# Whole-token stacks of queries and keys, a value product in one part, and a new spread of w_in's splitting steps

## The chip, the core and the metric

The kernel runs on one core of one Trainium2 chip, with its five engines: PE (matrix products, with PEld for the loading of weights), DVE (vector), ACT (scalar functions), POOL (a second, slower vector engine) and SP, which here only issues transfers. The metric is the device time of one launch in microseconds (us). Three runs of the kernel before took 1129.81, 1126.02 and 1126.63 us, median 1126.63. Trace times below count from the start of the profiled span.

## The reference

One block of a network on x of 2048 tokens by 640 features: attention with a sliding window of 256 tokens and 32 heads of 20 features, and then a gated mixer.

```python
def _A_ref(x, wqkv, wo):
    H = 32; Dh = D // H; W = 256
    qkv = (x @ wqkv) as [3, B, H, S, Dh]
    scores = einsum("bhqd,bhkd->bhqk", q, k) * Dh ** -0.5
    mask = (idx[:, None] - idx[None, :] >= 0) & (idx[:, None] - idx[None, :] < W)
    p = softmax(where(mask, scores, -1e9))
    return einsum("bhqk,bhkd->bhqd", p, v) as [B, S, D] @ wo

def _B_ref(x, w_in, w_sp, b_sp, w_out):
    z = gelu(x @ w_in); z1 = z[..., :864]; z2 = layernorm(z[..., 864:])
    g = w_sp @ z2 + b_sp[:, None]
    return (z1 * g) @ w_out

h = x + _A_ref(layernorm(x), wqkv, wo)
h2 = h + _B_ref(layernorm(h), w_in, w_sp, b_sp, w_out)
```

## The kernel before, in words

**Stages.** The first 60 us hold the layer norm and v. From there to about 237 us come the dense products for queries and keys (`qk_item`, products on L568 to L570): each 128 x 512 result is split into three bf16 parts (L584 to L592, the splits of which DVE, ACT and POOL make one each) and stored to DRAM as `qk_d` (L595). From 238 to about 470 us runs the attention loop, from 466 to 558 us the 16 iterations of the product with wo, and then the mixer's products, up to the end.

**Stacks.** The heads stand in 8 groups of 4. For a group `load_stack` (L298) makes a *stack*: 120 partitions with six copies of bf16 parts of 20 features, so that one bf16 product over 120 rows gives a score that is nearly f32, and three further rows (120 to 122) that carry the negative row maxima on the side of the queries and ones on the side of the keys. A stack is two tiles, one for each half of the tokens (`b`). Each holds queries (`a` = 0) and keys (`a` = 1) of the four heads. There are three slots for stacks, `slot_0` (first slot), `slot_1` (second) and `xb`; in names of the order below the pairs of tiles are `slot_0_99`, `slot_1_100`; `slot_0_1950`, `slot_1_1951`; `xb_94`, `xb_95`, the half b = 0 first. 24 loads (L311: half b, part j, side a, in this nesting) fill a stack. The ones are set by POOL (L304), for the first three groups only.

**The attention loop** has steps s = 0 to 129, 16 for each group. For each of the four heads of a step s, in this order: `max_item(s + 16)` makes the product of 128 queries with their window of keys in four strips (L341) for the row maxima, which DVE takes (L351); `score_item(s)` makes 128 keys by 384 queries (L394), here with the maxima's rows in the product, and ACT takes the exponential (L397), POOL masks it (L401, L404); and `pv_item(s - 2)` makes the product with v and the row sum (L422) in two parts, the first after head 1, the second after head 3. Every second step its result is evicted (L438 on ACT, L440 on DVE) and stored to `o_d` (L441). So group g's maxima are made in the 16 steps before its scores; for group 0 in the dense stage, there as a single product of 128 queries (L345).

**The maxima's way.** After 8 query blocks `max_rows` transposes 32 columns of maxima on PE (L357), which DVE and POOL split in three bf16 rows; SP stores them to `m_d` (L366) and loads them into rows 120 to 122 of the stack (L368). For the second token half of group g that begins in step 16g, after head 1.

**What sets the order.** PE, DVE, ACT and SP take their instructions in the written order of the program; a tile framework adds the waits, from which tile an instruction reads or writes and where. SP issues nearly all transfers, each in its turn. In the wo loop (L1300 on) a generator `w1` makes one splitting step of w_in for each `next`, one an iteration and a second one where a list of iterations says so.

Of the kernel before, what the change touches and what calls it, by code (L numbers as in the profile page):

```python
# [7 lines left out]
F32 = mybir.dt.float32  # L8
F32R = mybir.dt.float32r
BF16 = mybir.dt.bfloat16  # L10
# [5 lines left out]
P = 128  # L16
S = 2048
D = 640
H = 32
DH = 20  # L20
# [8 lines left out]
ONES = 1.0019378662109375  # L29
# [5 lines left out]
def block_kernel(ctx, tc, x, xt, wqk, wv, wo, w_in, wsp, bsp, w_out, out):  # L35
    nc = tc.nc
# [201 lines left out]
    with ExitStack() as ab:  # L238
# [14 lines left out]
        slot_w, slot_ap = {}, {}  # L253

        def add_slot(i, halves):

            slot_ap[i] = [h.bitcast(BF16).rearrange("p (a h t) -> p a h t", a=2, h=4) for h in halves]
# [40 lines left out]
        def load_stack(g):  # L298


            st = slot_w[g % 3]
            if g < 3:
                for h in st:
                    nc.gpsimd.memset(h[96:P, 1], ONES)  # L304
                    if g == 2:
                        yield
            for b in range(2):
                for j, parts in enumerate(((0, 0), (0, 1), (0, 2), (1, 0), (1, 1), (2, 0))):
                    for a in range(2):
                        src = qk_d[g // 4, parts[a], b, a * DH:(a + 1) * DH, g % 4 * 4:g % 4 * 4 + 4]  # L310
                        nc.sync.dma_start(st[b][j:6 * DH:6, a], src)  # L311
# [11 lines left out]
        def one(st, rows, a, hh, t0, n):  # L323
            (_, _, x), = tokens(st, rows, a, hh, t0, n)
            return x

        def max_item(g, qb, hh, strips=True):

            st = slot_ap[g % 3]
            ps = s1_tile()  # L330
            lo = max(0, qb - 2) * P
            n = (qb + 1) * P - lo
            keep = mask[:, 384 - n:]
            if strips:
                skip = 32 if qb > 1 else 0
                if skip:
                    n, keep = 288, strip
                for j in range(4):
                    q0 = qb * P + 32 * j
                    for o, w, k in tokens(st, 120, 1, hh, lo + skip * j, n):  # L340
                        nc.tensor.matmul(ps[32 * j:32 * j + 32, o:o + w], one(st, 120, 0, hh, q0, 32), k,  # L341
                                         start=True, stop=True, tile_position=(0, 32 * j))
            else:
                for o, w, k in tokens(st, 120, 1, hh, lo, n):
                    nc.tensor.matmul(ps[:, o:o + w], one(st, 120, 0, hh, qb * P, P), k, start=True, stop=True)  # L345
            b, c = divmod(qb, 8)
            if c == 0 and hh == 0:
                m_cols[g, b] = tmp2.tile([P, 32], F32, tag="mcol", bufs=2, name=f"mcol{g}_{b}")
            junk = tmp2.tile([P, 384], BF16, tag="junk", bufs=2, name=f"junk{g}_{qb}_{hh}")
            c += hh * 8  # L350
            nc.vector.tensor_tensor_reduce(out=junk[:, :n], in0=ps[:, :n], in1=keep, scale=1.0,  # L351
                                           scalar=NEG, op0=OP.add, op1=OP.max, accum_out=m_cols[g, b][:, c:c + 1])

        def max_rows(g, b):

            ps = s1_tile()[:32, :P]
            nc.tensor.transpose(ps, m_cols.pop((g, b)), ident)  # L357
# [8 lines left out]
            nc.sync.dma_start(rows.rearrange("a r c -> r a c"), m3.bitcast(F32))  # L366
            yield
            nc.sync.dma_start(slot_w[g % 3][b][120:123, 0], rows.rearrange("a (h r) c -> a h (r c)", h=4))  # L368
            yield

        p_tiles, pv_tiles = {}, {}
# [1 line left out]
        def score_item(u, hh):  # L373


            g, kb = divmod(u, NT)
            st = slot_ap[g % 3]
            n = min(384, S - kb * P)
            if hh == 0:
                p_tiles[u] = tmp3.tile([P, 4, 384], F32, tag="pt", bufs=4, name=f"pt{u}")  # L380
            pt = p_tiles[u]
            if u > NU - LEAD:
                if hh % 2 == 0:
                    bank2.append(bank2.pop(0))
                ps = bank2[-1][:, hh % 2]
            else:
                ps = s2_tile()
            for i in range(4):
                k0 = kb * P + 32 * i
                b, e = 32 * i, min(n, 32 * i + 288)  # L390
                if NU - LEAD < u and 4 * (u - NU + LEAD - 1) + hh < 6:
                    b, e = 0, n
                for o, w, q in tokens(st, 123, 0, hh, kb * P + b, e - b):
                    nc.tensor.matmul(ps[32 * i:32 * i + 32, b + o:b + o + w], one(st, 123, 1, hh, k0, 32), q,  # L394
                                     start=True, stop=True, tile_position=(0, 32 * i))
            if u <= NU - LEAD:
                nc.scalar.activation(pt[:, hh, :n], ps[:, :n], AF.Exp, scale=SCALE)  # L397
# [46 lines left out]
        if True:  # L444
# [134 lines left out]
            def split_qk(m, c, ps):  # L579
                sg = tmp.tile([P, 3, 512], BF16, tag="ta", bufs=3, name=f"sg{m}_{c}")  # L580
                rest = tmp.tile([P, 512], F32, tag="tb", bufs=2, name=f"rest{m}_{c}")
                nc.vector.tensor_tensor(out=rest, in0=ps, in1=stds[c], op=OP.mult)
                yield
                nc.scalar.activation(sg[:, 0, :], rest, AF.Copy)  # L584
                yield
                (nc.gpsimd if m > 5 else nc.vector).tensor_tensor(out=rest, in0=rest, in1=sg[:, 0, :],
                                                                  op=OP.subtract)
                if (m, c) == (9, 3):
                    nc.gpsimd.tensor_copy(out=sg[:, 1, :], in_=rest)
                else:  # L590
                    nc.scalar.activation(sg[:, 1, :], rest, AF.Copy)
                nc.gpsimd.tensor_tensor(out=sg[:, 2, :], in0=rest, in1=sg[:, 1, :], op=OP.subtract)  # L592
                T = S // 4
                base = qk_d[m // 5, 0, c // 2, m % 5 * 8, 0, c % 2 * 256:c % 2 * 256 + 256]
                nc.sync.dma_start(bass.AP(tensor=base.tensor, offset=base.offset,  # L595
                                          ap=[[T, P], [2 * 2 * DH * H // 2 * T, 3], [1, 256]]), sg.bitcast(F32))

            halves = [slice(0, HD), slice(HD, D)]
            load_x(0)
# [711 lines left out]
    for i in range(1, NT + 1):  # L1311
# [95 lines left out]
```

## Time and profile before

| what | value |
|---|---|
| median of 3 runs | 1126.63 us |
| profiled execution | 1125.76 us |
| its span | 1124.0 us |
| PE busy | 1089.4 us, 97% |
| DVE / ACT / POOL busy | 752.8 / 567.5 / 319.6 us |
| matrix products on L341, L394, L422 | 1280, 1296 and 1984 in the costliest forms |
| transfers in q1 | 87,536 packets, 178.74 MB |

Rows of PE, DVE, ACT and POOL name an instruction by line and by tiles, `out<-in`; `SPq` rows are transfers at the moment of their issue, not their landing. A "timeline" row gives start, duration and a count of like instructions. A row of the waits gives an engine, its waiting line, `<-` the engine, tile and line that it waited for, and the sum, the number and the longest of these waits. "issue" stands for time in which an engine waited for nothing that the profile shows.

### The profile page before, as it was taken

To read this page: it belongs to the slowest core of one execution; us is meant where nothing else is said; L and a number is where in the kernel's file an instruction comes from. 1 tells how busy PE (TensorE), PEld (TensorE's weight loads), DVE (VectorE), ACT (ScalarE), POOL (GpSimd) and SP (SyncE) were. 2 spreads that over 40 slices of the span, in tenths; PEclk is the share of its full clock that TensorE was granted. 3 is DMA by queue.
4 is the path that set the end of the run, shared out by engine and by line. 5 is a ranking of instruction groups with operands and counts; after the bars stand their busy time and mean duration, and the time that the engine had idled before them with its cause. 6 is when DMAs were issued, how large, how long until landed. Compare 5 with 4: busy or idle time off the path is not lost.

```text
span 1124.0 us, 28713 instructions
## 1 busy us (share of the span) xinstructions
PE 1089.4 (97%) x11139; PEld 980.3 (87%) x11139; DVE 752.8 (67%) x2070; ACT 567.5 (50%) x1155; POOL 319.6 (28%) x447
## 2 busy tenths in 40 slices
PE   8999999989999999999999999999999999999998
PEld 8998887657877777699899999999999899999998
DVE  6643444779988999588877678655358974556542
ACT  4444443248988899735566567434347521222210
POOL 4324446766766666723200011000001000000000
PEclk9999999989999999999999999999999999999999
DMA  7834567545555555689554522242251563444321
GB/s 256 283 113 135 171 186 248 183 157 181 179 179 172 177 178 165 170 249 311 218 195 167 182 91 76 75 134 90 104 171 57 180 209 119 124 148 148 98 87 60
DMA packets 87672, 180.57 MB, mean 161 GB/s; under 512 B 11440, under 2 KB 45760, under 8 KB 83648
## 3 DMA queue, kind: packets, MB, share of 16 engines
q1 hardware_dynamic: 87536, 178.74, 49.8%
q8 instruction: 87, 1.43, 0.5%
q14 instruction: 49, 0.40, 0.1%
HBM read 120.82 MB, written 57.88 MB: 159 GB/s over the span
## 4 chain that ended last, share of the span: by engine, by line
PE 72%; DMA 8%; ACT 7%; DVE 6%; issue 3%; POOL 2%; SPq 1%; DVEq 0%; POOLq 0%; ACTq 0%
PE g L1136 22%; PE out_ps L1201 8%; ACT pt L397 5%; PE pv L422 4%; PE zb L1028 4%; PE qk L568 3%; PE qk L569 3%; PE qk L570 3%; PE bank L341 3%; PE bank L394 3%; PE zx L976 2%; PE zv L976 2%; PE zy L976 1%; PE wo_ps L101 1%; DMA o_d<-ot 1%
## 5 line engine op out<-in xcount | busy, mean ns | idle before, releaser
L397 ACT ACTIVATE pt<-bank 128x384 f32<-128x384 f32 (+1 forms) x452 | 180.1, 478 | 26.4 <-PE bank L394 16.2
L803 ACT ACTIVATE aw<-fx 128x512 fp32r<-128x512 f32 (+2 forms) x160 | 93.7, 596 | 173.5 <-PE g L1136 120.7
L1136 PE MATMUL g<-zl,aw 128*128 128x432 f32 x768 | 171.0, 358 | 0.0
L351 DVE CUSTOM_DVE_ANT_0 junk<-bank,strip 128x288 bf16<-128x288 f32 x392 | 156.7, 454 | 16.3 <-PE bank L341 13.8
L1136 PEld LDWEIGHTS g<-zl,aw 128*128 128x128 f32 x768 | 143.6, 188 | 5.9
L422 PE MATMUL pv<-pt,v_sb 128*32 128x192 f32 (+3 forms) x1984 | 129.6, 323 | 6.2 <-ACT ot L438 3.8
L1136 PE MATMUL g<-ze,aw 128*128 128x432 f32 x576 | 134.0, 360 | 0.3 <-DVE row L797 0.2
L797 DVE TENSOR_TENSOR aw<-fx,aw 128x512 fp32r<-128x512 f32 (+2 forms) x160 | 102.7, 647 | 37.1 <-ACT aw L803 35.8
L1136 PEld LDWEIGHTS g<-ze,aw 128*128 128x128 f32 x576 | 107.0, 188 | 6.7 <-ACT aw L803 1.2
L401 POOL TENSOR_SCALAR_AFFINE_SELECT pt<-pt 128x512 f32<-128x512 f32 x128 | 83.9, 656 | 62.7 <-ACT pt L397 60.2
L394 PE MATMUL bank<-slot 123*32 123x288 bf16 (+7 forms) x1296 | 94.4, 276 | 4.9 <-ACT pt L397 3.5
L1201 PE MATMUL out_ps<-wout,y_sp 128*128 128x320 f32 (+1 forms) x630 | 96.2, 309 | 0.4 <-ACT y_sp L140 0.4
L341 PE MATMUL bank<-slot 120*32 120x288 bf16 (+6 forms) x1280 | 92.2, 277 | 3.6 <-issue 1.6
L1028 PE MATMUL zb<-win,aw 128*128 128x432 f32 x480 | 95.4, 359 | 0.0
L1201 PEld LDWEIGHTS out_ps<-wout,y_sp 128*128 128x128 f32 (+1 forms) x630 | 94.1, 188 | 1.2 <-ACT y_sp L140 0.7
L87 POOL TENSOR_TENSOR mvz<-mvz,half 128x1 f32<-128x1 f32 x16 | 10.1, 633 | 298.8 <-DVE mvz L86 296.8
L1028 PEld LDWEIGHTS zb<-win,aw 128*128 128x128 f32 x480 | 89.9, 187 | 5.0 <-ACT row L803 0.3
L422 PEld LDWEIGHTS pv<-pt,v_sb 128*32 128x32 f32 x1984 | 59.9, 110 | 18.1 <-issue 9.9
L797 DVE TENSOR_TENSOR row<-g,row 128x432 f32<-128x432 f32 x80 | 48.2, 604 | 37.8 <-PE g L1136 36.9
L394 PEld LDWEIGHTS <-slot 123*32 123x32 bf16 x1728 | 58.5, 97 | 15.3 <-issue 6.0
L404 POOL TENSOR_SCALAR_AFFINE_SELECT pt<-pt 128x512 f32<-128x512 f32 x112 | 71.4, 637 | 0.0
L351 DVE CUSTOM_DVE_ANT_0 junk<-bank,mask 128x384 bf16<-128x384 f32 (+2 forms) x120 | 51.7, 447 | 21.1 <-PE bank L345 15.8
(196 smaller groups left out, 2247.1 us busy)
## 6 DMA issues: line engine op xcount, KB each, us to landing
slot<-qk_d SPq DMA_DIRECT2D x144, 160.0 KB
fx<-wsp_in SPq DMA_DIRECT2D x32, 512.0 KB
qk_d<-sg SPq DMA_DIRECT2D x40, 384.0 KB
fx<-hn_d SPq DMA_DIRECT2D x32, 320.0 KB
o_d<-ot SPq DMA_DIRECT2D x64, 128.0 KB
xb<-qk_d SPq DMA_DIRECT2D x48, 160.0 KB
z_d<-row SPq DMA_DIRECT2D x16, 432.0 KB
g_d<-row SPq DMA_DIRECT2D x16, 432.0 KB
```

Source lines behind the costliest of these rows:

```text
L341: nc.tensor.matmul(ps[32 * j:32 * j + 32, o:o + w], one(st, 120, 0, hh, q0, 32), k, start=True, stop=True, tile_position=(0, 32 * j))
L351: nc.vector.tensor_tensor_reduce(out=junk[:, :n], in0=ps[:, :n], in1=keep, scale=1.0, scalar=NEG, op0=OP.add, op1=OP.max, accum_out=m_cols ...
L394: nc.tensor.matmul(ps[32 * i:32 * i + 32, b + o:b + o + w], one(st, 123, 1, hh, k0, 32), q, start=True, stop=True, tile_position=(0, 32 * i))
L397: nc.scalar.activation(pt[:, hh, :n], ps[:, :n], AF.Exp, scale=SCALE)
L401: nc.gpsimd.affine_select(out=pt[:, :, :P], in_=pt[:, :, :P], pattern=[[0, 4], [1, P]], base=0, channel_multiplier=-1, compare_op=OP.is_ge ...
L404: nc.gpsimd.affine_select(out=pt[:, :, 256:], in_=pt[:, :, 256:], pattern=[[0, 4], [-1, P]], base=-1, channel_multiplier=1, compare_op=OP. ...
L422: nc.tensor.matmul(ps[32 * hh:32 * hh + 32, a - 512 * c:b - 512 * c], v_sb[:, kb, v0:v0 + 32], pt[:, hh, a - kb * P:b - kb * P], start=fir ...
L797: (eng or nc.vector).tensor_tensor(out=out, in0=a, in1=b, op=op)
L803: nc.scalar.activation(out, a, AF.Copy)
L1028: nc.tensor.matmul(b[0][:, :HF], a[t][:, x, kk], win2[0][:, y, kk, h * HF:(h + 1) * HF], start=kk + x + y == 0, stop=kk == KD - 1 and x == 1)
L1136: nc.tensor.matmul(ps, w[m][:, x, k], zc[k][m][:, y], start=start and k + x + y == 0, stop=stop and k == 3 and x == 1, skip_group_check=True)
L1201: nc.tensor.matmul(ps[j][:, :HD], src[:w, a, k, :], e1["wout"][:w, b, k, j * HD:(j + 1) * HD], start=(k == 0 and a + b == 0), stop=(k == K ...
```

## The change

1. **Stacks by side, not by half.** The two tiles of a slot become one of queries and one of keys, each with all 2048 tokens of four heads. `qk_d` is laid out so that a head's tokens stand in one piece. A load still brings one half of the tokens of one part and one side, in the same nesting, but now as four pieces of 2 KB a row in place of one of 8 KB. The ones go to the tile of keys, by two fills of two heads. The maxima go to the tile of queries. A window across token 1024 no longer needs two products.
2. **The value product** is cut where a bank of 512 columns ends, and nowhere else. Where no bank ends within the 384 columns it is a single part, made after head 1, and the eviction and store that follow it come after head 1 too.
3. **w_in's splitting steps**: the second `next` comes in iterations 5, 7 and 9 in place of 4 and 6.

```diff
-    qk_d = dram.tile([2, 3, 2, 2 * DH, H // 2, S // 4], F32, name="qk_d")
+    qk_d = dram.tile([2, 3, 2 * DH, H // 2, S // 2], F32, name="qk_d")
...
-            slot_w[i] = [h.bitcast(F32).rearrange("p (a h t) -> p a h t", a=2, h=4) for h in halves]
+            slot_w[i] = [h.bitcast(F32).rearrange("p (h t) -> p h t", h=4) for h in halves]
...
-            st = slot_w[g % 3]
+            st, T = slot_w[g % 3], S // 4
             if g < 3:
-                for h in st:
-                    nc.gpsimd.memset(h[96:P, 1], ONES)
+                for i in range(2):
+                    nc.gpsimd.memset(st[1][96:P, 2 * i:2 * i + 2], ONES)
                     if g == 2:
                         yield
             for b in range(2):
                 for j, parts in enumerate(((0, 0), (0, 1), (0, 2), (1, 0), (1, 1), (2, 0))):
                     for a in range(2):
-                        src = qk_d[g // 4, parts[a], b, a * DH:(a + 1) * DH, g % 4 * 4:g % 4 * 4 + 4]
-                        nc.sync.dma_start(st[b][j:6 * DH:6, a], src)
+                        t = slice(b * T, (b + 1) * T)
+                        src = qk_d[g // 4, parts[a], a * DH:(a + 1) * DH, g % 4 * 4:g % 4 * 4 + 4, t]
+                        nc.sync.dma_start(st[a][j:6 * DH:6, :, t], src)
                         yield
...
-            o = 0
-            while o < n:
-                c, t = divmod(t0 + o, S // 2)
-                w = min(n - o, S // 2 - t)
-                yield o, w, st[c][:rows, a, hh, t:t + w]
-                o += w
+            return st[a][:rows, hh, t0:t0 + n]
...
-                    for o, w, k in tokens(st, 120, 1, hh, lo + skip * j, n):
-                        nc.tensor.matmul(ps[32 * j:32 * j + 32, o:o + w], one(st, 120, 0, hh, q0, 32), k,
-                                         start=True, stop=True, tile_position=(0, 32 * j))
+                    nc.tensor.matmul(ps[32 * j:32 * j + 32, :n], tokens(st, 120, 0, hh, q0, 32),
+                                     tokens(st, 120, 1, hh, lo + skip * j, n),
+                                     start=True, stop=True, tile_position=(0, 32 * j))
...
-            nc.sync.dma_start(slot_w[g % 3][b][120:123, 0], rows.rearrange("a (h r) c -> a h (r c)", h=4))
+            t = slice(b * S // 4, (b + 1) * S // 4)
+            nc.sync.dma_start(slot_w[g % 3][0][120:123, :, t], rows.rearrange("a (h r) c -> a h (r c)", h=4))
...
-            mid = (a // 512 + 1) * 512 if a // 512 < (e - 1) // 512 else a + 192
+            mid = min(e, (a // 512 + 1) * 512)
...
-        if i in (4, 6):
+        if i in (5, 7, 9):
             next(w1, None)
```

**In the built programs.** The lines L311, L341, L357, L366, L368, L394, L441 and L595 are L312, L331, L348, L357, L360, L385, L433 and L587 after the change. On PE, the first products of group 3's maxima (step 32), before:

```order
L422 MATMUL pv_3_4156<-pt_4169,v_sb 32x192 x3
L341 LDWEIGHTS slot_0_99 [waits DMAHW4_49,DMAHW5_49,DMAHW3_49,DMAHW7_49,DMAHW1_49,DMAHW0_49]
L341 MATMUL bank_118<-slot_0_99 32x128 [waits DVE_49]
...
L394 LDWEIGHTS xb_94 [waits DMAHW7_49]
L394 MATMUL bank_119<-xb_94 32x288 [waits Activation_49]
...
L394 MATMUL bank_119<-xb_94 32x256 [waits Activation_49]
L394 LDWEIGHTS xb_94
L394 MATMUL bank_119<-xb_95,xb_94 32x32 [waits DMAHW2_49]
```

The first row waits for loads of the first half alone (`slot_0_99`), by the counts in the program. The score products of group 2 follow; the last row, in step 38, is the first that reads its second half (`xb_95`), and there stands the wait for the second rows of maxima. The same places after:

```order
L331 LDWEIGHTS slot_0_99 [waits DMAHW5_49,DMAHW4_49,DMAHW6_49,DMAHW3_49,DMAHW7_49,DMAHW1_49,DMAHW0_49]
L331 MATMUL bank_118<-slot_1_100,slot_0_99 32x128 [waits DVE_49]
...
L385 LDWEIGHTS xb_95 [waits DMAHW7_49]
...
L331 MATMUL bank_117<-slot_1_100,slot_0_99 32x288
L385 LDWEIGHTS xb_95 [waits DMAHW2_49]
L385 MATMUL bank_119<-xb_94,xb_95 32x288 [waits Activation_49]
```

By the counts, the lanes in the first row are now those of all loads of keys, the 24th of the stack among them. The wait for the second rows of maxima (DMAHW2_49) has moved from step 38 to step 34, head 1, 149 rows behind the group's first score row, where it was 409 before.

On SP, around the same time, before:

```order
L311 DMA slot_1_100<-qk_d 20x2048 x3
L441 DMA o_d<-ot_2_1_4218 128x256
L311 DMA slot_1_100<-qk_d 20x2048 x3
L441 DMA o_d<-ot_3_0_4332 128x256
L311 DMA slot_0_1950<-qk_d 20x2048
L366 DMA m_d<-m_2_1_4361 32x3x64
L311 DMA slot_0_1950<-qk_d 20x2048 x2
L441 DMA o_d<-ot_3_1_4429 128x256
L368 DMA xb_95<-m_d 3x2048
```

and after:

```order
L433 DMA o_d<-ot_2_1_4022 128x256
L312 DMA slot_1_100<-qk_d 20x4x512
L312 DMA slot_0_99<-qk_d 20x4x512
L312 DMA slot_1_100<-qk_d 20x4x512
L433 DMA o_d<-ot_3_0_4105 128x256
L312 DMA slot_0_1950<-qk_d 20x4x512
L357 DMA m_d<-m_2_1_4157 32x3x64
L312 DMA slot_1_1951<-qk_d 20x4x512
L312 DMA slot_0_1950<-qk_d 20x4x512
L433 DMA o_d<-ot_3_1_4221 128x256
L360 DMA xb_94<-m_d 3x4x512
```

SP's order is the same; the stack's last three loads stand between the stores of `ot_2_1` and `ot_3_0`, and the last of the three is one of keys (`slot_1_100`) in both. The store and the reload of the maxima keep their places too.

On POOL, at the end of the dense stage, before:

```order
L304 MEMSET xb_94 32x2048
L586 TENSOR_TENSOR rest_2_2140<-rest_2_2140,sg_2_2139 128x512
...
L592 TENSOR_TENSOR sg_3_2265<-rest_3_2266,sg_3_2265 128x512
L304 MEMSET xb_95 32x2048
L586 TENSOR_TENSOR rest_3_2308<-rest_3_2308,sg_3_2307 128x512
```

and after:

```order
L578 TENSOR_TENSOR rest_3_2258<-rest_3_2258,sg_3_2257 128x512
L304 MEMSET xb_95 32x2048
L584 TENSOR_TENSOR sg_3_2257<-rest_3_2258,sg_3_2257 128x512
L304 MEMSET xb_95 32x2048
L578 TENSOR_TENSOR rest_3_2300<-rest_3_2300,sg_3_2299 128x512
```

Both fills now write the tile of keys and stand next to the last but one split; the first stood four splits earlier.

More of the change, by code (lines that the diff above doesn't have):

```diff
@@ L255, in add_slot @@
         def add_slot(i, halves):
-            slot_ap[i] = [h.bitcast(BF16).rearrange("p (a h t) -> p a h t", a=2, h=4) for h in halves]
-            slot_w[i] = [h.bitcast(F32).rearrange("p (a h t) -> p a h t", a=2, h=4) for h in halves]
+            slot_ap[i] = [h.bitcast(BF16).rearrange("p (h t) -> p h t", h=4) for h in halves]
+            slot_w[i] = [h.bitcast(F32).rearrange("p (h t) -> p h t", h=4) for h in halves]
         add_slot(0, s0)
@@ L309, in load_stack @@
                     for a in range(2):
-                        src = qk_d[g // 4, parts[a], b, a * DH:(a + 1) * DH, g % 4 * 4:g % 4 * 4 + 4]
-                        nc.sync.dma_start(st[b][j:6 * DH:6, a], src)
+                        t = slice(b * T, (b + 1) * T)
+                        src = qk_d[g // 4, parts[a], a * DH:(a + 1) * DH, g % 4 * 4:g % 4 * 4 + 4, t]
+                        nc.sync.dma_start(st[a][j:6 * DH:6, :, t], src)
                         yield
         def tokens(st, rows, a, hh, t0, n):
-            o = 0
-            while o < n:
-                c, t = divmod(t0 + o, S // 2)
-                w = min(n - o, S // 2 - t)
-                yield o, w, st[c][:rows, a, hh, t:t + w]
-                o += w
-        def one(st, rows, a, hh, t0, n):
-            (_, _, x), = tokens(st, rows, a, hh, t0, n)
-            return x
+            return st[a][:rows, hh, t0:t0 + n]
         def max_item(g, qb, hh, strips=True):
@@ L339, in max_item @@
                     q0 = qb * P + 32 * j
-                    for o, w, k in tokens(st, 120, 1, hh, lo + skip * j, n):
-                        nc.tensor.matmul(ps[32 * j:32 * j + 32, o:o + w], one(st, 120, 0, hh, q0, 32), k,
-                                         start=True, stop=True, tile_position=(0, 32 * j))
-            else:
-                for o, w, k in tokens(st, 120, 1, hh, lo, n):
-                    nc.tensor.matmul(ps[:, o:o + w], one(st, 120, 0, hh, qb * P, P), k, start=True, stop=True)
+                    nc.tensor.matmul(ps[32 * j:32 * j + 32, :n], tokens(st, 120, 0, hh, q0, 32),
+                                     tokens(st, 120, 1, hh, lo + skip * j, n),
+                                     start=True, stop=True, tile_position=(0, 32 * j))
+            else:
+                nc.tensor.matmul(ps[:, :n], tokens(st, 120, 0, hh, qb * P, P), tokens(st, 120, 1, hh, lo, n),
+                                 start=True, stop=True)
             b, c = divmod(qb, 8)
@@ L392, in score_item @@
                     b, e = 0, n
-                for o, w, q in tokens(st, 123, 0, hh, kb * P + b, e - b):
-                    nc.tensor.matmul(ps[32 * i:32 * i + 32, b + o:b + o + w], one(st, 123, 1, hh, k0, 32), q,
-                                     start=True, stop=True, tile_position=(0, 32 * i))
+                nc.tensor.matmul(ps[32 * i:32 * i + 32, b:e], tokens(st, 123, 1, hh, k0, 32),
+                                 tokens(st, 123, 0, hh, kb * P + b, e - b),
+                                 start=True, stop=True, tile_position=(0, 32 * i))
             if u <= NU - LEAD:
@@ L592, in split_qk @@
                 nc.gpsimd.tensor_tensor(out=sg[:, 2, :], in0=rest, in1=sg[:, 1, :], op=OP.subtract)
-                T = S // 4
-                base = qk_d[m // 5, 0, c // 2, m % 5 * 8, 0, c % 2 * 256:c % 2 * 256 + 256]
+                T = S // 2
+                base = qk_d[m // 5, 0, m % 5 * 8, 0, c * 256:c * 256 + 256]
                 nc.sync.dma_start(bass.AP(tensor=base.tensor, offset=base.offset,
-                                          ap=[[T, P], [2 * 2 * DH * H // 2 * T, 3], [1, 256]]), sg.bitcast(F32))
+                                          ap=[[T, P], [2 * DH * H // 2 * T, 3], [1, 256]]), sg.bitcast(F32))
             halves = [slice(0, HD), slice(HD, D)]
```

## The prediction

> **What bounds the kernel now.** First comes the page's header, then the windows of the two stages that the change touches (dense projections, attention), then the waits of the attention stage.
>
> ```profile
> span 1124.0 us, 28713 instructions
> 200.00:210.00 10.00, 10.00 (x47) 6.28 (x45) 7.52 (x25) 2.54 (x5) 8.18 (x6) 1.00 0.46 146
> 308.00:336.00 28.00, 25.11 (x762) 20.75 (x766) 24.30 (x125) 23.71 (x63) 18.11 (x32) 1.00 0.57 173
> ACT pt L397 <- PE bank L394: 16.2, 41, 2.3
> PEld pv L422 <- issue: 9.7, 20, 0.6
> PEld L394 <- issue: 9.1, 11, 3.3
> PEld L341 <- issue: 5.5, 10, 1.8
> PE pv L422 <- ACT ot L438: 3.8, 14, 0.3
> ```
>
> A windows row gives length, then busy time and count of PE, PEld, DVE, ACT and POOL, then the granted clock, DMA share and GB/s. PE is full in the dense stage and busy 25.1 of 28 us in attention; ACT (23.7) is close behind, but the waits are of ACT on PE (16.2 us). PE's own idle time there is mostly "issue" (9.7 + 9.1 + 5.5 = 24.3 us between 240 and 470 us) and 3.8 us for the eviction of the value product. So whatever stops PE in these stages is paid almost in full, since its instructions go strictly in order and nothing behind it has slack to give back.
>
> **What the change adds: waits.** The built program shows more than the diff. Each stack was two tiles by token halves, each with queries and keys; it is now one tile of queries and one of keys. Two waits move forward with that, and in the program they stand on PE.
>
> *A, the first product of queries and keys of a group.* It waited for the loads of the first half; now its semaphores include the last of the group's 24 loads, which was needed eight steps later. When does that load land?
>
> ```profile
> 184.99 2.20 SPq L311 DMA_DIRECT2D slot<-qk_d  x3
> 298.62 2.20 SPq L311 DMA_DIRECT2D slot<-qk_d  x3
> 359.04 2.20 SPq L311 DMA_DIRECT2D xb<-qk_d  x3
> 183.29 0.23 PE L345 MATMUL bank<-slot 120*128 120x128 bf16 x1
> 300.62 0.23 PE L341 MATMUL bank<-slot 120*32 120x128 bf16 x4
> 361.08 0.23 PE L341 MATMUL bank<-xb 120*32 120x128 bf16 x4
> 208.58 3.04 DMA slot<-qk_d
> 217.93 3.77 DMA slot<-qk_d
> ```
>
> Three loads issue in 2.20 us, so the last of them starts 1.47 us after the row: at 186.46, 300.09 and 360.51. The chain of waits has such loads landing 3.04 to 3.77 us after issue; I take 3.6, as these are last in a full queue. They land at 190.06, 303.69 and 364.11, and PE comes to the product at 183.29, 300.62 and 361.08. The wait is 6.8 us in the dense stage (group 0) and 3.1 and 3.0 us at the two starts in the loop. Six groups start so: 6 x 3.1 = 18.6, and with the 6.8 **25 us**. Behind the waiting product stand PE's scores, so ACT starves, and DVE has no products to reduce. Group 1 starts where the dense stage ends; PE stands there soon after anyway, for the first exponentials (under moved work), so I take nothing.
>
> *B, the score product at step 2 of each group, head 1.* The rows of maxima of the second token half were needed at step 6, where the keys' window first crosses token 1024. In one tile, head 1's queries stand behind head 0's second half, and the program makes the product of step 2, head 1 wait for that second transfer.
>
> ```profile
> 301.26 0.28 PE L357 MATMUL bank<-ident,mcol 128*32 128x128 f32 x1
> 303.11 0.32 SPq L366 DMA_DIRECT2D m_d<-m  x1
> 306.87 0.27 SPq L368 DMA_DIRECT2D xb<-m_d  x1
> 304.36 0.31 PE L394 MATMUL bank<-xb 123*32 123x288 bf16 x4
> 363.58 0.33 SPq L366 DMA_DIRECT2D m_d<-m  x1
> 366.43 0.27 SPq L368 DMA_DIRECT2D slot<-m_d  x1
> 364.83 0.31 PE L394 MATMUL bank<-slot 123*32 123x288 bf16 x4
> 303.11 3.70 DMA m_d<-m
> 321.89 2.33 DMA o_d<-ot
> ```
>
> The rows are transposed on PE in step 0 (301.26), stored from 303.11 (3.70 us to land) and reloaded from 306.87. For the reload the nearest chain row is a short transfer of 2.33 us, so they are in at 309.20; the product is due at 304.36, 4.8 us earlier. In the next pair of rows: 366.43 + 2.33 = 368.76 against 364.83, 3.9 us. A's wait doesn't shorten this one, because the transpose stands behind A too. Mean 4.35 for six groups: 26 us, less about 0.3 each that ACT still has queued: **24 us**. Group 0's rows come from the dense stage and are near in time; I take 1.5 us there (0 to 4).
>
> For the last group, at the tail, the same wait stands two steps in:
>
> ```profile
> 450.33 0.87 PE L394 MATMUL pair<-slot 123*32 123x384 bf16 x16
> 452.21 0.27 SPq L368 DMA_DIRECT2D slot<-m_d  x1
> ```
>
> 452.21 + 2.33 = 454.54 against about 450.7: 3.8 us. ACT is further behind here and PE has slack, so **2 us**.
>
> **The clock** after such stops. The records show it halved twice around this stage:
>
> ```profile
> 243.80:247.22 3.42, 3.42 (x64) 2.60 (x60) 2.67 (x12) 3.42 (x9) 2.12 (x4) 0.51 0.42 134
> 546.77 0.53 PE L101 MATMUL wo_ps<-xb 128*128 128x320 f32 x2 [1.85 <-DVE xh L1299]
> 547.59:551.00 3.41, 3.41 (x15) 3.41 (x14) 3.28 (x8) 1.20 (x2) 1.47 (x2) 0.51 0.37 145
> 245.25 0.48 PE L394 MATMUL bank<-slot 123*32 123x288 bf16 x4
> 245.73 0.48 PE L394 MATMUL bank<-slot 123*32 123x288 bf16 x4
> 248.08 0.30 PE L394 MATMUL bank<-slot 123*32 123x288 bf16 x4
> 248.33 0.30 PE L394 MATMUL bank<-slot 123*32 123x288 bf16 x4
> ```
>
> An idle stretch of 1.85 us before 546.77 was followed by 3.41 us at 0.51. At half clock a score item with its product takes 0.48 us (245.25 to 245.73), at full clock 0.25 (248.08 to 248.33), so one such stretch loses about 3.4 x (1 - 0.25/0.48) = 1.6 us. There are 13 long stops (A at seven places, B at six). Some of the halved stretch falls in the stop itself, some stops lie across two stretches: I take 0.8 us each, **10 us** (0 to 21).
> The Trainium skill (TensorE: Matmul & The Clock Gate, "HAM oscillation — how this bites in real kernels") has the clock fall only when an idle gap exceeds about 3.4 us. By that rule most stops of A would keep the clock, and the sum would be some 6 us lower; the 1.85 us gap above speaks against it, so the row decides.
>
> **What it removes.** 488 narrow products with their weight loads go, as no window is cut at token 1024 any more, and 288 of the value products, as 384 columns now go in one part where no bank ends. The columns streamed stay the same. Two sorts of idle time can go with them. One is instruction supply; its longest stops stand in steps with split windows, such as this one:
>
> ```profile
> 317.11 0.31 PE L394 MATMUL bank<-xb 123*32 123x288 bf16 x4 [2.35 <-issue]
> 315.29 1.82 issue
> ```
>
> If the 9% fewer instructions remove a part of the 24.3 us of issue, I take -5 (0 to -12). The other is the wait for the eviction (3.8 us), which now comes two heads earlier in the step, so that its bank is asked for later: -2 (0 to -4). The merged product itself: -1 (0 to -3). What is won between step 8, whose store and reload of maxima hold SP's queue, and step 16 is partly eaten by A, because the last load then still lands when it did: +2. Sum **-6 us**.
>
> **Moved work.** The two fills of ones now both go to the tile of keys, one of them late in POOL's queue, ahead of the last split that the first exponentials wait for:
>
> ```profile
> 237.54 1.80 POOL L304 MEMSET xb<- 32x2048 f32 x1
> ACT pt L397 <- POOL sg L592: 4.2, 1, 4.2
> ```
>
> That is up to 1.8 us more on a chain for which ACT already waits 4.2 us; I take +1 (0 to 1.8). The splitting steps of w_in go one iteration later or earlier within the wo loop: 0 (-2 to +2), hidden behind that loop's loads. If that cover goes, one step (a copy on ACT and a difference on DVE) stands ahead of the next normalisation.
>
> **The loads themselves** go from 20 pieces of 8 KB to 80 of 2 KB. What that does to their issue no row shows. Two neighbours:
>
> ```profile
> 99.91 0.37 SPq L595 DMA_DIRECT2D qk_d<-sg  x1
> 292.66 0.36 SPq L441 DMA_DIRECT2D o_d<-ot  x1
> ```
>
> The store of the split queries has 384 pieces of 1 KB and issues in 0.37 us, the present load 0.73 with only 20. So pieces alone don't set the price, and it may fall to 0.37 or rise; I leave it at 0.73. Nine loads are issued between the reload of the maxima at step 8 and the group's start, so each 0.1 us moves A by up to 0.9 us per group.
>
> **Sum:** 25 (A) + 24 + 1.5 + 2 (B) + 10 (clock) - 6 + 1 = 57.5 us. The profiled execution had 1124.0 us of span and 1125.76 us in all, 0.9 under the median of the runs, 1126.63. A little of A overlaps with stops of supply that would have come anyway (3 us), so I forecast 1126.6 + 54, about **1180 us**, with 1158 to 1202 as this case's own range: the clock's and the issue's bounds, -10 and +11, and B0, supply and w_in another 8 or so.
>
> **Rivals.**
> *The loads issue faster.* At 0.37 us the nine loads end 3.2 us sooner: the six starts in the loop lose their 18.6 us with their clock stops (5), and A in the dense stage falls to perhaps 5. For it: the store's row. Against it: the load has its own odd pattern (every sixth row of the tile), which stays. B remains: 1180 - 18.6 - 5 - 2 = about 1154 us.
> *The loads issue slower.* With four times the pieces, 1.1 us each would make 24 loads 26.4 us of a group that now takes 29; the nine before the start end 3.3 us later: 6 x 3.3 + 3 for the dense stage: about 1203 us, more if landing grows too. SP becomes a second bound; the price decides from about 1.0 us on.
> *The waits are covered and the removed instructions win.* If the waits that the program lists were met when PE arrives, only -6 - 2 (w_in) would stay, with up to -12 of supply: 1108 to 1121, say 1116 us, faster than before. It would need the last load 3 us and the maxima 4 us sooner, at all groups. The only lever is PE falling behind for another reason; nothing in the queue of SP shows such room.
> *The change does nothing:* gains and half-covered waits cancel within 3 us.
>
> **How the numbers follow.** Forecast case 0.60, faster issue 0.20, slower issue 0.11, covered 0.06, nothing 0.03. The range 1142 to 1208 holds the first two whole and most of the third. About 0.3% (3.4 us) is what a measurement can tell from no change: faster 0.06, the same 0.03, slower 0.91.
>
> **What would show it.** In the profile after, PE waits on the loads of queries and keys at the first product of each group, near 3 us at six places and near 7 once, and on the reload of the maxima at step 2, near 4 us at six places; the windows around them show clocks under 1.00; the dense stage ends some 8 us later; an attention group takes about 37 us, not 29. If the row of the loads has 0.37 us, the first rival is right; if 1.0 and more, the second. The forecast is wrong if PE's waits in 240 to 520 us for these two transfers sum to under 25 us, or if the wo iterations change by more than 4 us.

## The result, and the profile after

The changed kernel takes 1210.62 us (median of 5 runs, 1209.1 to 1211.57) against 1129.81 us before in the same comparison: a ratio of 1.0723, 95% interval 1.0702 to 1.0743. The prediction of 1180 us had the sign, the places and the mechanism of the waits, but the time lies 2.6 us above the wider of its two ranges (1142 to 1208 us; 1158 to 1202 for its own case).

The header and the shares of the changed kernel:

```profile
span 1208.9 us, 26532 instructions
PE 1117.5 (92%) x10075; PEld 969.1 (80%) x10075; DVE 757.3 (63%) x2070; ACT 570.3 (47%) x1155; POOL 315.1 (26%) x447
```

PE has 9.6% fewer products than before (10075 against 11139) and is yet busy 28 us longer. Nothing in the products became longer by design, so this busy time is time at a lower clock (the mean granted clock is 0.960, against 0.995 before). The waits of PE between 180 and 560 us (engine, line, releaser; sum, number, longest):

```profile
PE bank L331 <- DMA slot<-qk_d: 16.4, 3, 5.7
PE bank L331 <- DMA xb<-qk_d: 9.5, 2, 4.8
PE bank L331 <- DMA o_d<-ot: 4.8, 1, 4.8
PE bank L335 <- DMA slot<-qk_d: 7.2, 1, 7.2
PE bank L385 <- DMA slot<-m_d: 14.2, 5, 3.4
PE bank L385 <- DMA xb<-m_d: 6.6, 2, 3.6
PE pair L385 <- DMA slot<-m_d: 4.4, 1, 4.4
```

The kernel before had none of these but 1.0 us of the first kind. They are the waits A (L331, six of 4.7 to 5.7 us, 30.7 us in sum; L335, 7.2 us in the dense stage) and B (L385, one in group 0 and six behind it, 20.8 us in sum; one more at the tail, 4.4 us). One row of A goes to the store `o_d<-ot`; it stands at the same instruction as the other five and is the same wait, named after the transfer that came last in the profile.

One group start of the changed kernel, from PE's timeline (A at 330.94, B at 340.01) and from SP's:

```profile
325.56 0.26 PE L385 MATMUL bank<-slot,slot 123*32 123x32 bf16 x4
330.94 0.30 PE L331 MATMUL bank<-slot,slot 120*32 120x128 bf16 x4 [5.12 <-DMA slot<-qk_d]
340.01 0.43 PE L385 MATMUL bank<-xb,xb 123*32 123x288 bf16 x4 [3.58 <-DMA xb<-m_d]
```

```profile
317.67 0.73 SPq L360 DMA_DIRECT2D xb<-m_d  x1
325.34 2.40 SPq L312 DMA_DIRECT2D slot<-qk_d  x3
336.99 0.73 SPq L360 DMA_DIRECT2D xb<-m_d  x1
```

And the windows around both stops, cut at the clock's own steps (busy time of PE, PEld, DVE, ACT, POOL, then the granted clock):

```profile
325.52:328.93 3.41, 0.30 (x16) 0.06 (x4) 0.87 (x6) 0.72 (x3) 0.63 (x1) 0.99 0.61 206
328.93:332.34 3.41, 1.41 (x21) 0.76 (x25) 0.69 (x5) 0.74 (x2) 0.00 (x0) 0.50 0.40 129
332.34:335.76 3.42, 3.42 (x64) 2.45 (x60) 2.37 (x12) 1.95 (x6) 1.92 (x4) 0.51 0.09 18
335.76:339.17 3.41, 0.67 (x20) 0.33 (x12) 1.41 (x8) 1.18 (x3) 1.22 (x2) 0.99 0.46 136
339.17:342.58 3.41, 2.57 (x32) 1.33 (x36) 0.55 (x3) 0.81 (x2) 0.00 (x0) 0.50 0.44 145
342.58:346.00 3.42, 3.42 (x52) 1.82 (x48) 2.08 (x9) 2.48 (x7) 1.22 (x2) 0.51 0.00 2
```

Here a stretch in which PE is idle for most of its 3.41 us (0.30 and 0.67 us busy) is followed by two stretches at half clock, not one. Taking the transposes of the maxima in the trace as marks, a group takes 39.8 us (238.7 us for six), against 29.4 before (176.4). From there the account of the loss: 62 us in these six groups, 14 us before them, 7 us at the tail, and hardly any after it: the first product with wo starts 83.3 us later (553.9 against 470.6 us) and the 16 iterations take 87 us in both kernels.

### The profile page after: what moved, and what is told of

The parts are those of the page before. It is cut to its first block, busy times and chain, and to the rows that moved or that the text cites. A ratio compares the mean times of both kernels' runs of the same rounds, so it can differ in the third digit from the quotient of the medians.

```text
span 1208.9 us, 26532 instructions
## 1 busy us (share of the span) xinstructions
PE 1117.5 (92%) x10075; PEld 969.1 (80%) x10075; DVE 757.3 (63%) x2070; ACT 570.3 (47%) x1155; POOL 315.1 (26%) x447
## 4 chain that ended last, share of the span: by engine, by line
PE 42%; DMA 6%; DVE 4%; ACT 2%; issue 1%; SPq 1%; POOL 1%; DVEq 0%; ACTq 0%; POOLq 0%
PE g L1128 20%; PE out_ps L1193 8%; PE zb L1020 4%; PE zx L968 2%; PE zv L968 2%; PE zy L968 1%; PE wo_ps L101 1%; PE zw L968 1%; PE yt_ps L1182 1%; DMA rs<-r_d 1%; DMA fx<-wsp_in 1%; DMA m<-o_d 1%; DMA wraw<-w_in_in 1%; DVE zl L789 1%; DVE row L789 1%
## 5 line engine op out<-in xcount | busy, mean ns | idle before, releaser
L414 PE MATMUL pv<-pt,v_sb 128*32 128x384 f32 (+2 forms) x1408 | 123.0, 424 | 2.1 <-POOL pt L396 1.5
L331 PE MATMUL bank<-slot,slot 120*32 120x288 bf16 (+2 forms) x1280 | 97.3, 309 | 21.7 <-DMA slot<-qk_d 10.8
L385 PE MATMUL bank<-slot,slot 123*32 123x288 bf16 (+5 forms) x1296 | 98.2, 309 | 19.1 <-DMA slot<-m_d 14.2
L385 PEld LDWEIGHTS <-slot 123*32 123x32 bf16 x1536 | 53.0, 106 | 51.6 <-issue 25.4
L331 PEld LDWEIGHTS <-slot 120*32 120x32 bf16 x1280 | 44.4, 106 | 44.3 <-issue 26.5
```

What stands on the lines that cost most here:

```text
L331: nc.tensor.matmul(ps[32 * j:32 * j + 32, :n], tokens(st, 120, 0, hh, q0, 32), tokens(st, 120, 1, hh, lo + skip * j, n), start=True, stop= ...
L385: nc.tensor.matmul(ps[32 * i:32 * i + 32, b:e], tokens(st, 123, 1, hh, k0, 32), tokens(st, 123, 0, hh, kb * P + b, e - b), start=True, sto ...
L414: nc.tensor.matmul(ps[32 * hh:32 * hh + 32, a - 512 * c:b - 512 * c], v_sb[:, kb, v0:v0 + 32], pt[:, hh, a - kb * P:b - kb * P], start=fir ...
```

## The experiments

In what follows, theory W is that of the prediction: waits A and B, and the clock they halve. Marks and group times are worked out from the traces as above.

### Each part alone

```diff
  pv_alone, before:
-            mid = (a // 512 + 1) * 512 if a // 512 < (e - 1) // 512 else a + 192
+            mid = min(e, (a // 512 + 1) * 512)
  win_alone, before:
-        if i in (4, 6):
+        if i in (5, 7, 9):
  stack_alone, the change: both of these undone
```

> Only the value product in one part where no bank ends, stacks and w_in as before. Theory W (the added waits A and B, with the clock they halve, are the whole loss): 1118 to 1127 us, since none of these waits is added and 288 products go. Rival V (the single part, 0.65 us in one piece ahead of the scores, starves the exponentials): 1135 us or more, with more waits of ACT on PE's scores.

> Only the new spread of w_in's splitting steps. Theory W: 1124 to 1129 us, no difference. Rival S (the spread collides with the wo iterations): some 5 us slower, all of it between 470 and 560 us.

> Only the whole-token stacks, value product in two parts and w_in as before. Theory W: 1203 to 1220 us, within 1% of the whole change, with the same stops of PE of 5 us at six group starts and 3 us two steps later. If V holds instead, it falls well under 1190 us.

Measured: 1125.62 us (ratio to before 0.9992, 0.9970 to 1.0014), 1128.30 us (0.9998, 0.9977 to 1.0019) and 1212.06 us (1.0759, 1.0714 to 1.0803). The whole loss is that of the whole-token stacks; the other two parts can't be told from no change.

### Wait A taken away from the change, and put into the kernel before

```diff
  keys_first, the change:
-                for j, parts in enumerate(((0, 0), (0, 1), (0, 2), (1, 0), (1, 1), (2, 0))):
-                    for a in range(2):
+                for a in (1, 0):
+                    for j, parts in enumerate(((0, 0), (0, 1), (0, 2), (1, 0), (1, 1), (2, 0))):
  a_in_before, the kernel before:
-            for b in range(2):
+            for b in (1, 0) if g else (0, 1):
```

> The whole change, but within each token half the six loads of keys go ahead of the six of queries (the first products of a group wait for all loads of keys, but for queries only of the first half), so the last load waited for is issued six loads earlier, 5 us or so. Theory W: A goes, with 32 us of stops in the loop, some 6 us in the dense stage and most of the halved clock behind them: 1130 to 1155 us, B unchanged. Rival Q (smaller pieces make the queue of SP the bound): the same number of loads of the same kind, so 1190 us or more.

> The kernel before, with nothing but the order of the halves turned round in the loads of groups 1 to 7: second half first. The first product of a group then waits for the last load, as wait A does, without stacks by side, single value products, small pieces or wait B. Theory W: six stops of 3.5 to 5 us in the loop with their halved clock, 1148 to 1168 us. If the whole-token tile itself is the loss, it stays within 5 us of the kernel before.

`keys_first` took 1183.39 us (ratio 1.0507, 1.0461 to 1.0553): 27 us of the loss went, and not the 55 to 80 expected. A is gone from the loop, but B grew: its seven stops in the loop sum to 33.1 us, against 20.8. One of them, which was 3.58 us in the change:

```profile
331.42 0.43 PE L385 MATMUL bank<-xb,xb 123*32 123x288 bf16 x4 [4.90 <-DMA xb<-m_d]
```

B's end is set by the way of the maxima (transpose, store, reload), which counts from the transpose: from there to the product that waits are 7.4 to 8.3 us in the six groups of the change, and 7.7 to 8.3 in four of the six groups here (9.6 and 9.9 in the others). So whatever PE loses between the transpose and step 2, to the clock after A for one, B gives back. Without A, PE comes to B sooner and waits longer. The dense stop stayed (7.4 us).

`a_in_before` took 1161.19 us (1.0273, 1.0244 to 1.0302), within its bounds. A by itself, in the old tiles with the old pieces and products, costs 33 us:

```profile
310.11 0.30 PE L341 MATMUL bank<-slot 120*32 120x128 bf16 x4 [3.85 <-DMA slot<-qk_d]
```

Six stops of 3.3 to 5.4 us sum to 23.8 us in its trace; the rest is put down to the halved clock (34.5 us a group against 29.4 before, and 4.0 us of the difference are the stop; the granted clock is 0.92 in these groups, against 1.00).

### The size of the pieces

```diff
  halves_2kb, the kernel before with the new layout of qk_d:
+                        t = slice(b * S // 4, (b + 1) * S // 4)
+                        src = qk_d[g // 4, parts[a], a * DH:(a + 1) * DH, g % 4 * 4:g % 4 * 4 + 4, t]
...
```

> The kernel before, with only the layout of queries and keys in DRAM changed, so that each load brings four pieces of 2 KB a row as in the change, into the old half-token tiles. Theory W: no wait is added, the load issues in 0.75 us, 1124 to 1131 us. Rival Q (the pieces load SP and the transfer engines): 1140 us or more, with PE waiting on loads.

Measured 1126.66 us, ratio 0.9995 (0.9971 to 1.0020). Four times the pieces, and the load's issue goes from 0.70 to 0.75 us:

```profile
L311 SPq DMA_DIRECT2D slot<-qk_d x144: 694/702/1885, 160.1 to 418.1; - x144
```

```profile
L312 SPq DMA_DIRECT2D slot<-qk_d x144: 745/752/1832, 161.1 to 419.2; - x144
```

The first row is of the kernel before, the second of this run (minimum, median, maximum in ns). Rival Q falls.

### Wait B taken away

```diff
  rows_by_head, the change:
-            nc.sync.dma_start(slot_w[g % 3][0][120:123, :, t], rows.rearrange("a (h r) c -> a h (r c)", h=4))
+            for h in range(4):
+                nc.sync.dma_start(slot_w[g % 3][0][120:123, h, t], rows[:, 8 * h:8 * h + 8].rearrange("a r c -> a (r c)"))
  both: keys_first and rows_by_head together
  both_late: both, and the reload two steps later
-                if hh == 3 and u1 % 8 == 1 and s <= NU - LEAD + 1:
+                if hh == 3 and u1 % 8 == 3 and s <= NU - LEAD + 3:
  both_late_two: both_late with the value product in two parts
```

> The whole change, but the reload of the maxima goes as four transfers, one per head, so that no product waits for rows of another half (in the program the second rows are waited for at step 6 again). Theory W: B goes (20 us of stops in the loop, 2.6 at its head, 4.8 at the tail, and the halved clock behind them), A stays and grows by a microsecond or so per group, since SP issues more ahead of a group's last load: 1175 to 1195 us. If B's stops were only a symptom of A, nothing changes: 1205 us or more.

> The whole change with keys first and the reload by head. Theory W: no stop of PE over 2 us in the loop, a group in 28 to 29 us as with the value product in one part alone, granted clock 1.00 there; only the dense stage's 7.8 us with its halved clock stays: 1128 to 1142 us. Rival Q (four times the pieces in SP's queue, reload in four): 1160 us or more, with SP late in every group.

> Keys first, reload by head, and the reload's place on SP two steps later, so that SP does not stand 1 to 1.7 us per reload until the store of the maxima has landed (it did in the run with keys first and reload by head, where stops of 2 to 3.7 us at group starts were left). Theory W: these stops shrink below 1.5 us, a group takes 28.2 to 29.5 us: 1127 to 1138 us. If SP has no room for other reasons, no change from 1146 us.

> The same with the value product in two parts again, so that what is left of the change is the whole-token stack without its waits. If the 488 products it removes cured the stops of instruction supply, a group takes 28.2 to 28.6 us as with the single value product; if the single value product did, 29 us or more and 5 to 8 us behind the run before it.

`rows_by_head`: 1173.53 us (1.0390, 1.0326 to 1.0453). B is gone, worth 37 us, with A grown to 4.7 to 7.8 us. No product reads other data than in the change; only the transfer is cut by head. So B was no wait for data: the product of step 2, head 1 waited for a transfer into tokens that it does not read. That the one transfer over four heads is taken by its first and last address would explain it, and why head 0 was spared, but no run shows the rule itself.

`both`: 1146.19 us (1.0147, 1.0083 to 1.0210), 64 us of the loss gone, but above the 1128 to 1142 expected. Stops of 1.9 to 3.5 us at five group starts were left:

```profile
312.27 0.30 PE L331 MATMUL bank<-slot,slot 120*32 120x128 bf16 x4 [2.70 <-DMA slot<-qk_d]
```

`both_late`: 1142.10 us (1.0104, 1.0077 to 1.0132). The stops at group starts went, and three of 2.2 to 3.4 us came back at the score products, as the second half's reload was now late itself; a wash, and above the bounds given. `both_late_two`: 1141.61 us (1.0097, 1.0074 to 1.0120). Its six groups take 175.3 us, about as many as before (176.4), with 488 products fewer, but with 6 us of stops at score products left in them. Neither expectation held whole: a group takes 29.2 us, but the run is no slower than the one before it. `halves_2kb` keeps all 488 and takes 172.1 us. So no run shows a gain of more than a few microseconds from the products that no longer cross token 1024.

### The head: the dense stop

```diff
  both_early, both, and group 0's last loads earlier in the dense stage:
-                if n % 5 == 4:
+                if n % 3 == 2 and n < 12:
...
  dense_late, both_late_two, and the first product of maxima later:
-            for n in range(20):
+            for n in range(27):
...
-                if n % 5 == 4:
+                if n % 5 == 4 and n < 20:
```

> As the run with keys first and reload by head, and the second half of group 0's loads stands some nine microseconds earlier in the dense stage. Theory W: the stop of 7.8 us at the first dense product goes too, and with it its halved clock: 1116 to 1130 us, even with the kernel before or a little under. If the dense stage has slack elsewhere, no better than the run without it.

> As the run with keys first, reload by head and later, value product in two parts, and the first product of maxima in the dense stage comes seven dense pieces (some 7 to 9 us) later, when group 0's loads have landed. Theory W: the stop of 8 us there goes, with up to 10 us at halved clock behind it; some maxima are left over without dense products beside them at the stage's end (up to 3 us): 1130 to 1136 us from 1141.6. If the head's loss is not that stop, 1140 us or more.

`both_early` (1144.69 us, 1.0124, 1.0049 to 1.0199) missed: the loads hardly came earlier. In SP's timeline the last twelve still come between 176 and 187 us (in the change between 175 and 188), since SP issues with few breaks from 160 us on; between 165 and 190 us it stands for no more than 2.4 us:

```profile
176.27 4.76 SPq L312 DMA_DIRECT2D slot<-qk_d  x6
181.60 2.34 SPq L312 DMA_DIRECT2D slot<-qk_d  x3
184.55 2.36 SPq L312 DMA_DIRECT2D slot<-qk_d  x3
```

`dense_late` moved the product instead and took 1130.60 us (1.0039, 1.0018 to 1.0061), 11 us less than the run that it builds on, or 6.5 by the two ratios to the kernel before. The stop of 8.0 us became 3.5:

```profile
191.99 0.22 PE L335 MATMUL bank<-slot,slot 120*128 120x128 bf16 x1 [3.53 <-DMA qk_d<-sg]
```

In the trace the loop's first transpose comes 8.2 us earlier (261.3 against 269.5). With this, all but 4 us of the 80 are taken back, with whole-token stacks and their layout kept; the value product is in two parts here.

### The clock

```diff
  fill_ab, the change, with products that nobody reads (`fill`) ahead of the waits:
...
+                if u1 < NU and s and s % NT == 0 and hh == 0:
+                    fill(1, 22)
...
+                if 2 < s < NU - LEAD and s % NT == 2 and hh == 1:
+                    fill(2, 12)
```

> The whole change, and in each of the six groups' stops PE makes products that nobody reads: 22 of identity by identity ahead of the wait A (4.7 us at full clock), 12 ahead of the wait B (2.6 us). The waits stay; only the clock can change. Theory W: the granted clock in the loop rises from 0.84 to near 1.00; what that is worth is bounded, since the time at half clock behind A is partly spent in B's wait anyway: 7 to 25 us less than the whole change, 1185 to 1204 us. If the clock is no part of the loss, 1210 us or more.

Measured 1203.77 us (1.0651, 1.0583 to 1.0719), 7 us less than the change, a gain at the lower edge of the 7 to 25 us expected. From 300 to 500 us, the change and this run, and then one group start of this run:

```profile
300.00:500.00 200.00, 158.93 (x3482) 107.99 (x3478) 138.43 (x683) 134.14 (x343) 98.30 (x170) 0.86 0.42 130
```

```profile
300.00:500.00 200.00, 189.16 (x3966) 145.52 (x3969) 140.60 (x709) 137.14 (x356) 102.38 (x176) 0.98 0.44 133
```

```profile
327.16 5.18 PE L365 MATMUL bank<-ident 128*128 128x128 f32 x44
333.59 0.24 PE L331 MATMUL bank<-slot,slot 120*32 120x128 bf16 x4 [1.25 <-issue]
337.39 2.94 PE L365 MATMUL bank<-ident 128*128 128x128 f32 x24
342.49 0.31 PE L389 MATMUL bank<-xb,xb 123*32 123x288 bf16 x4 [2.15 <-DMA xb<-m_d]
```

The clock is back (0.86 to 0.98) and buys little, since PE at full clock only comes sooner to a wait whose end does not move: the filling and the rest of the wait are 6.4 us at A and 5.1 us at B. So at full clock the two waits alone are some 11 us in this group, as much as a group of the change loses in all (39.8 against 29.4). In three of the six groups the filling lasts as long as wait A or longer, with no idle time behind it, so 7 us may be too low for what the clock is worth.

### Where the single value product's gain went

```diff
  pv_not_tail, the kernel before:
-            mid = (a // 512 + 1) * 512 if a // 512 < (e - 1) // 512 else a + 192
+            mid = (a // 512 + 1) * 512 if a // 512 < (e - 1) // 512 or u < NU - LEAD else a + 192
```

> The kernel before with the value product in one part in groups 0 to 6 and in two parts in the last group. In the profiles the loop's six groups took 171.1 us with the single part against 176.4, and the tail, from the last single score to the first wo product, 22.5 us against 20.5. If both are the single part's doing, 1120 to 1125 us, under the kernel before; if the loop's gain is only the chance of instruction supply, as the 172.1 us of the kernel with small pieces alone suggest, 1125 to 1129 us.

Measured 1124.41 us (12 runs), ratio 0.9974 (0.9958 to 0.9989): the one run here that beats both kernels, by a quarter of a percent. With the single part everywhere, the loop gains and the tail loses, by the profiles: the six groups take 171.1 us in `pv_alone` and 169.4 here, against 172.1 to 177.8 in three programs with two parts (`halves_2kb`, the kernel before, `win_alone`). From the last single score to the first wo product take 20.5 us before, 22.5 us in `pv_alone`, 20.5 us here. The waits of that stretch, of `pv_alone` and of this run:

```profile
PEld pv L422 <- POOL pt L404: 5.0, 10, 1.2
PEld pv L422 <- POOL pt L401: 2.6, 6, 0.7
```

```profile
PEld pv L422 <- POOL pt L401: 5.1, 11, 1.0
```

A part of all 384 columns needs POOL's second masking (L404), one of the first 192 only the first (L401). In the tail, where no product of maxima fills PE, that is on the path.

## Why the prediction was wrong

**What bounds the kernel: right.** PE paid for its stops in full, and the loss lies where PE was full.

**Wait A: right in place and number, too small.** 18.6 us were forecast for the six starts and 6.8 for the dense stage; the waits show 30.7 and 7.2. The step that failed is the price of what stands in SP's queue between the reload of the maxima and the last load. In the kernel before, this reload is issued at

```profile
292.29 0.27 SPq L368 DMA_DIRECT2D xb<-m_d  x1
```

and the last load 7.8 us later, at 300.09. In the change it is 9.3 us (317.67 to 326.94, the third of the loads of 325.34). Of the 1.5 us more, 0.46 are the reload, which went from 0.27 to 0.73 us of issue as it turned from one piece per row to four, and which the prediction never priced. Another 0.55 are the eight loads between, each less than 0.1 us slower, and 0.49 are the stores, one of which took 0.85 us. The landing took 4.0 us against the 3.6 taken, and PE came 0.2 us sooner. Together that makes 5.1 us against 3.1.

**Wait B: right in mechanism; its size depends on what stands ahead.** 4.05 us net per group were forecast; the six groups show 3.1, and group 0 2.2 where 1.5 was taken. The reload took longer than forecast (336.99 to 340.01, 3.0 us against 2.33), but PE, at half clock behind A, came later still; with the clock full B is 5.1 us in the group shown. At the tail, "ACT is further behind here and PE has slack" failed: 4.4 us against 2.

**The clock: about right as a cost, for the wrong reason.** Forecast were 0.8 us a stop, 10 us in all. In fact a stop mostly halves two stretches, and PE is busy 28 us longer with a tenth fewer products; but giving the clock back in the loop gave only some 7 us, as B swallows what PE gains. The prediction added A, B and the clock as independent terms, and they are not.
The Trainium skill's rule (TensorE: Matmul & The Clock Gate, "HAM oscillation — how this bites in real kernels") of an idle gap over 3.4 us agrees with A (gaps of 4.7 to 5.7 us) but not with B: six of its seven gaps in the loop were shorter, and the clock fell all the same, as behind the gap of 2.29 us ahead of 498.29, where the stretch from 499.60 ran at 0.51. The prediction had decided by the row, rightly.

**What it removes: mostly wrong.** -6 us were credited, and the total shows none of it. One premise was misread: the 24.3 us of "issue" stand in rows of PEld, the loading of weights, which overlaps with the products. PE itself was idle for 16.7 us between 240 and 470 us, and only 5.9 of them were issue. That part does go with the products: over the six groups PE waits 2.8 to 6.1 us for issue in three programs that have them all (`halves_2kb`, the kernel before, `win_alone`), and 0 to 0.7 us in three without the 488 (`stack_alone`, `both_late_two`, `dense_late`). But ahead of a stop whose end does not move, such a gain only brings PE sooner to the stop. The six groups take 238.7 us in the change and 238.5 in `stack_alone`, so the single value product gains nothing there, and the 175.3 us of `both_late_two` still hold 6 us of stops. At the tail the single value product loses 2 us, and the prediction did not see that wait: the single part needs a second masking. It credited the eviction's earlier place, which is real (PE's 3.8 us of waits for it are gone in `pv_alone`), but not what the earlier place asks of POOL.

**Moved work** went as said: w_in made no difference, and the first exponentials' wait grew from 4.2 to 5.6 us, forecast +1.

**The overlap credit of 3 us** is borne out by no run.

In sum, by the waits of the trace: A was short by 12.5 us (37.9 against 25.4) and the tail by 2.4, while B was 4.7 too high (20.8 against 25.5, both with group 0). The other terms (clock, removal, moved work, overlap) were forecast at 2 us together; what the waits leave of the loss of 81 us is 18. Nine of these 16 us are the credits for removal and overlap that did not come. The rest is not split by any run; the half clock is the only cause seen for it. Together this is 26 of the 30 us from 1180 to 1210; 3 more are the kernel before, which took 1129.81 us in this comparison and not 1126.63.

What stays open: why the iterations of wo take 85 to 87 us behind a single value product and 87 to 89 behind two parts, so that part of a gain in the loop is lost or kept there; and why the first dense product waits for queries of the second half at all, which a product of 32 queries in the loop does not.

## What to carry to other kernels

When two tiles become one, read the waits of the built program before the products saved: a product can come to wait for a transfer into parts of the new tile that it does not read, and an engine that works in strict order turns that into a stop of everything behind. Price every transfer whose shape the new layout changes, the small ones on the critical path above all; and do not add stops that end at a fixed event as if they were independent, since the later one takes back what the earlier ones lose. An order of loads by need, and one transfer for each unit that is waited for, took back 64 of 81 us here without touching the layout.

## What the hardware showed that had not been expected

The reload of the maxima issues in 0.27 us as 3 rows in one piece, in 0.73 us as 3 rows in four pieces, and in 0.26 us again as one head's 3 pieces:

```profile
L361 SPq DMA_DIRECT2D slot<-m_d x48: 253/266/367, 230.1 to 471.7; - x48
```

That is the run `both`, where four such transfers take 1.2 us in SP's queue. The load, by contrast, rose only from 0.70 to 0.75 us for 80 pieces in place of 20. So here it was not the number of pieces that set the issue.

And the clock falls for a second stretch of 3.41 us even though PE worked 2.57 us of the first (339.17 to 342.58). Between 180 and 560 us the changed kernel has 16 such falls. In the 11 where PE was busy for up to 2.65 us of the first half-clock stretch, the second was halved too; in the five where it was busy for 3.04 us or more, it was not. So here the length of the half clock went with the work that PE had in its first stretch.
